# Opening of a fused attention and feed-forward kernel: the first two token tiles as one block, ten weight slices in plain float32 and six in two rounded parts

## The chip, the cores and the metric

The kernel runs on one core of one Trainium2 chip. The metric is the time of one execution on the device, in microseconds. The engines are named as in the profile: PE (TensorE, matmuls and transposes), PEld (its weight loads), DVE (VectorE), ACT (ScalarE), POOL (GpSimd), SP (the queue that issues nearly all transfers).

## The reference

For 8 batches and 8 heads with 512 local and 32 global tokens of width 64, global queries see all 544 keys; a local query sees the 32 global keys and the local keys at most 32 positions away. The result, with 8 x 64 = 512 columns and 8 x 544 = 4352 token rows, goes through a feed-forward layer of width 2048.

```python
s_g = scale * np.matmul(q_g, k_all.transpose(0, 1, 3, 2))
out_g = np.matmul(sm(s_g), v_all)
...
s_l = np.concatenate([s_lg, s_ll], axis=-1)          # s_ll masked to |i - j| <= 32
out_l = np.matmul(sm(s_l), np.concatenate([v_g, v_l], axis=2))
x = np.concatenate([out_g, out_l], axis=2).transpose(0, 2, 1, 3).reshape(B * S, H * D)
...
h = x @ w_in                                          # 512 -> 2048
out = (h * (1.0 / (1.0 + np.exp(-h)))) @ w_out        # 2048 -> 512
```

The weights come as 64-bit floats and are turned into 32-bit floats on the chip.

## The kernel before, in words

**Tiles and steps.** The 4352 rows are 34 token tiles of 128 rows (32 local ones, and two that collect the global rows of four batches each). A local tile takes two attention steps `k` (64 in all), each of four heads in two halves `i`. A step is scores (`sc`, L347), masked maximum (`mx`, L359), exponential (`ex`, L370), the reciprocal of the sum (`no`, L375 and L377), scaling of the probabilities (`sl`, L383 on DVE, L385 on ACT), transposes (`tu`, L419 plain, L421 of a rounded copy that a transfer makes, L391), copies out of them (`pt`, L433 on DVE, L435 on ACT), global probabilities put beside them (`pp`, POOL), values (`va`, L463), and the result copied to the layer's input tile (`xc`, L476; `xl` its rounding rest, L480). Global queries of a batch have their own chain: `gsc`, `gcp`, `gmx` (L262), `gex`, `gno` (L273), `gtu` (L291, L293), `pgt`, and for the first four steps `late` and `lc`.

**The layer.** Its 2048 inner columns are 16 slices `f`. The tiles form blocks (`SIZES`, 13 of them): 1, 1, 2 and then ten of 3. Blocks 0 and 1 run in plain float32: `one` (t, f) is four matmuls of 128 columns for one tile (L582), `th` the tanh (L586, ACT), `st` the rest of the activation (L592, DVE), `two` one matmul of 512 columns (L598). The trace shows each plain matmul as two instructions. From block 2 on, weights, inputs and inner values are split in a rounded upper and a lower part, and every product is the sum of three: upper by upper, and the two mixed ones. The first layer is twelve matmuls (L729) over all of a block's columns, the second three per tile (L751 to L753). Between them stand tanh (L735, ACT), L736 (DVE), the upper part (L738, ACT) and the lower part (L739, DVE). The second layer of a slice runs behind the first layer of the next one.

**Weights.** Each slice comes in two halves `w` (512 KB each, seven buffers), w_in's and then w_out's. A half is decoded by `js` (L186, DVE), `ja` (L182, ACT) and `jo` (L191, DVE), and split by `wh` (L209, ACT) and `wl` (L213, POOL).

**Order.** The opening's order over all engines is written out by hand in `START`, a list of words such as `sl3.1.0` (what, step, half, head pair). Each engine but PE is bound to the order in which it meets its words; PE's order is the program's. The words hold steps 0 to 8 of the attention, `w0` to `w31`, all of blocks 0 and 1 but the last `two` of both, the global chains of batch 0 and the scores and probabilities of batch 1, 24 matmuls that keep TensorE warm, and the splitting of slices 0 to 7. So it stands around the place of step 3:

```python
mx1.0 w5 ex0.1 mx1.1 w6 warm4 sc2 raw4 no0.0 raw5 ex1.0 no0.1 sl0.0.1 sl0.0.0 sl0.1.1 no1.0 sl0.1.0 warm5 tu0.0
...
sl2.0.0 no2.1 xc1 no3.0 warm2 tu2.0 sl2.1.1 sl2.1.0 one0.0 sl3.0.1 pt2.0 js2 sl3.0.0 js3 tu2.1 th0.0 pt2.1 tu3.0
ex3.1 st0.0 warm1 va2 js4 pt3.0 no3.1 ja2 js5 two0.0 sl3.1.1 xc2 jo2 sl3.1.0 ja3 js6 tu3.1 w9 one0.1 ja4 pt3.1
ja5 jo3 va3 th0.1 gcp0.0 jo4 w10 st0.1 xc3 one0.2 w11 jo5 ja6 gmx0.0 one1.0 w12 ja7 jo6 th0.2 two0.1 th1.0 ja8
```

After `START` the blocks from 2 on run slice by slice, and the remaining attention steps are put between their matmuls by due times: `at(k)` is the place of step `k` in the stream, `EARLY` how far ahead of it its predecessor's transposes stand (up to step 14), `ends` the places at which the blocks end, and `fill` moves on with every piece of the layer. `KF` (8) is the first step whose probabilities are rounded by a transfer before their transposes (`mv`, `st_move`, `g_move`). `AHEAD` (4) counts the first steps, which load queries and keys whole, with one transfer each (`st_load`); later ones use three.

Of the kernel before, what the change touches and what calls it, by code (L numbers as in the profile page):

```python
# [1 line left out]

# [45 lines left out]
raw0 raw1 v0 raw2 v1 w0 w1 raw3 v2 v3 warm6 sc0 g0.0.0 g0.0.1 w2 mx0.0 warm1 sc1 w3 g0.1.0 mx0.1 ex0.0 g0.1.1 w4  # L48
mx1.0 w5 ex0.1 mx1.1 w6 warm4 sc2 raw4 no0.0 raw5 ex1.0 no0.1 sl0.0.1 sl0.0.0 sl0.1.1 no1.0 sl0.1.0 warm5 tu0.0
js0 sl1.0.0 sl1.0.1 tu0.1 pt0.0 mx2.0 tu1.0 ex1.1 pt0.1 js1 warm1 va0 pt1.0 mx2.1 ja0 no1.1 sc3 ja1 sl1.1.1 jo0  # L50
xc0 sl1.1.0 jo1 w7 ex2.0 warm4 tu1.1 mx3.0 w8 gsc0.0 ex2.1 pt1.1 no2.0 va1 g1.0.0 ex3.0 mx3.1 g1.0.1 sl2.0.1
sl2.0.0 no2.1 xc1 no3.0 warm2 tu2.0 sl2.1.1 sl2.1.0 one0.0 sl3.0.1 pt2.0 js2 sl3.0.0 js3 tu2.1 th0.0 pt2.1 tu3.0
ex3.1 st0.0 warm1 va2 js4 pt3.0 no3.1 ja2 js5 two0.0 sl3.1.1 xc2 jo2 sl3.1.0 ja3 js6 tu3.1 w9 one0.1 ja4 pt3.1
ja5 jo3 va3 th0.1 gcp0.0 jo4 w10 st0.1 xc3 one0.2 w11 jo5 ja6 gmx0.0 one1.0 w12 ja7 jo6 th0.2 two0.1 th1.0 ja8
st0.2 w13 st1.0 gsc0.1 js7 gex0.0 js8 two1.0 jo7 gcp0.1 one1.1 gno0.0 w14 wh0.0 jo8 ja9 two0.2 wl0.0 w15 th1.1
gmx0.1 one1.2 wh0.1 st1.1 ja10 wl0.1 gtu0.0 js9 th1.2 js10 two1.1 gex0.1 st1.2 one0.3 jo9 pgt0.0 ja11 gno0.1
two1.2 w16 pp4.0 jo10 pp4.1 th0.3 ja12 late0 w17 one1.3 ja13 st0.3 v4 lc0 js11 wh1.0 gtu0.1 js12 th1.3 two0.3
jo11 wl1.0 ja14 pgt0.1 w18 one0.4 st1.3 jo12 ja15 pp5.0 late1 js13 th0.4 w19 two1.3 ja16 lc1 v5 st0.4 jo13 late2
wh1.1 two0.4 lc2 ja17 w20 wl1.1 js14 late3 js15 one1.4 jo14 wh2.0 lc3 w21 one0.5 jo15 th1.4 wl2.0 ja18 js16 sc4
w22 st1.4 th0.5 jo16 ja19 two1.4 raw6 st0.5 wh2.1 w23 mx4.0 two0.5 wl2.1 mx4.1 ex4.0 one1.5 js17 js18 ex4.1  # L60
one0.6 no4.0 jo17 sc5 th1.5 sl4.0.0 sl4.0.1 w24 st1.5 th0.6 tu4.0 raw7 no4.1 ja20 st0.6 two1.5 sl4.1.1 pt4.0
jo18 sl4.1.0 two0.6 js19 ja21 w25 mx5.0 tu4.1 ja22 one1.6 jo19 ex5.0 one0.7 pt4.1 w26 th1.6 mx5.1 ja23 va4 st1.6
th0.7 no5.0 ex5.1 st0.7 two1.6 pp5.1 v6 sl5.0.1 pp6.0 js20 xc4 two0.7 no5.1 sl5.0.0 xl4 sl5.1.0 one1.7 sl5.1.1
ja24 jo20 one0.8 ja25 js21 w27 th1.7 js22 tu5.0 ja26 st1.7 sc6 jo21 th0.8 pt5.0 two1.7 st0.8 w28 jo22 wh3.0 raw8
two0.8 js23 w29 wh3.1 wl3.0 mx6.0 one1.8 ja27 jo23 ex6.0 one0.9 wl3.1 mx6.1 w30 th1.8 tu5.1 js24 ja28 st1.8 sc7
pt5.1 th0.9 ex6.1 two1.8 st0.9 raw9 no6.0 jo24 wh4.0 two0.9 sl6.0.0 sl6.0.1 w31 wl4.0 one1.9 no6.1 ja29 js25
sl6.1.0 sl6.1.1 va5 jo25 th1.9 ja30 st1.9 one0.10 mx7.0 wh4.1 pp6.1 v7 mx7.1 xc5 pp7.0 two1.9 th0.10 wl4.1 xl5
ex7.0 one1.10 st0.10 js26 ex7.1 two0.10 no7.0 jo26 th1.10 one0.11 sl7.0.0 sl7.0.1 ja31 st1.10 tu6.0 no7.1 js27
th0.11 two1.10 pt6.0 sl7.1.1 st0.11 sl7.1.0 one1.11 jo27 wh5.0 js28 two0.11 th1.11 wl5.0 js29 wh5.1 st1.11 tu6.1
jo28 two1.11 pt6.1 wl5.1 one0.12 jo29 va6 js30 th0.12 wh6.0 js31 st0.12 one1.12 jo30 wh6.1 wl6.0 v8 xc6 jo31  # L70
two0.12 th1.12 xl6 pp7.1 tu7.0 st1.12 wl6.1 gsc1.0 pt7.0 two1.12 g1.1.0 gcp1.0 g1.1.1 tu7.1 gmx1.0 one0.13 wh7.0
pt7.1 one1.13 wh7.1 wl7.0 gex1.0 va7 th0.13 wl7.1 gno1.0 th1.13 gsc1.1 st0.13 xc7 xl7 two0.13 gcp1.1 st1.13
# [15 lines left out]
def attention_moe_kernel(ctx: ExitStack, tc: tile.TileContext, qk0_in, qk_in, v_in, gqk, wts, out):  # L88
# [122 lines left out]
    def w_rest(f, i):  # L211
        sl = slice(i * DM, (i + 1) * DM)
        nc.gpsimd.tensor_tensor(out=w_two[f][i], in0=w_32[f][:, sl], in1=w_hi[f][:, sl].bitcast(F32), op=ALU.subtract)  # L213
# [381 lines left out]
    def other(t, f):  # L595
        if f == 0:
            outs[t] = [ps_out.tile([P, DM], F32, tag=f"out{t}", name=f"out{t}")]
        nc.tensor.matmul(outs[t][0], g_slice(t, f), w_32[f][:, DM:], start=(f == 0), stop=(f == NF - 1))  # L598
# [121 lines left out]
    def first_layer(n, f):  # L720
        nt = SIZES[n] * P
        xh, xl = xblk[n]
        h = ps_h.tile([P, 512], F32, tag="h", name=f"h{n}_{f}")
        i = 0
        for c in range(NCC):
            wh = w_hi[f][:, c * P : (c + 1) * P]
            wl = w_lo[f][:, c * P : (c + 1) * P]
# [120 lines left out]
```

## Time and profile before

| | |
|---|---|
| median of three runs | 1013.99 us (1012.42 to 1014.07) |
| profiled execution | 1014.88 us |
| its span, first to last instruction | 1013.1 us |
| granted TensorE clock | 0.998 |
| first matmul of block 2 | 104.87 us after the span's start |
| PE, DVE, ACT, POOL busy | 1001.5, 492.4, 497.3, 85.6 us |

Times inside the profile are counted from the span's start. A TensorE instruction's duration holds its way through the array, which overlaps the next one's; the chain of work that ended last shows instead how far apart they stand. The bracket behind an instruction is idle time of its engine just before it, and what ended that.

### The profile page before, as it was taken

The page shows a single profiled execution, that of the slowest core. Times are in us where ns is not written, and L with a number is a line of the kernel's source. Part 1 is how long each engine was busy: PE and PEld are TensorE (multiplying, and loading weights), DVE is VectorE, ACT ScalarE, POOL GpSimd, SP SyncE. Part 2 cuts the span into 40 slices and gives each one's busy share as a digit, 9 for nine tenths or more (in the row PEclk, how much of TensorE's full clock was granted, in tenths as well). Part 3 has the DMA queues.
Part 4 walks back from the last instruction along what each step waited for, and adds up shares of the span by engine and source line. Part 5 has one row for each costly group of instructions (what it writes and reads, how often), then busy time and mean ns, then how long its engine had stood idle before and what let it go on. Part 6 is the DMA issues. An engine that isn't in the chain of part 4 may idle for free.

```text
span 1013.1 us, 17720 instructions
## 1 busy us (share of the span) xinstructions
PE 1001.5 (99%) x6280; PEld 860.8 (85%) x6280; DVE 492.4 (49%) x1634; ACT 497.3 (49%) x1332; POOL 85.6 (8%) x239
## 2 busy tenths in 40 slices
PE   8999999999999999999999999999999999999998
PEld 5776877888888888888888888888888888898997
DVE  6888455444544444453354444444444544433222
ACT  7776567444544554453354454445445543532322
POOL 1334054000000000000000000000000000000000
PEclk9999999999999999999999999999999999999999
DMA  9982434332423332332132333234224321300001
GB/s 338 348 283 81 156 105 154 127 104 92 132 84 117 103 110 86 112 114 68 46 126 89 116 95 110 93 114 135 71 81 146 102 82 58 106 32 1 32 1 32
DMA packets 85032, 110.97 MB, mean 110 GB/s; under 512 B 7760, under 2 KB 56144, under 8 KB 84944
## 3 DMA queue, kind: packets, MB, share of 16 engines
q1 hardware_dynamic: 84608, 109.38, 33.2%
q8 instruction: 50, 0.82, 0.3%
q10 hardware_dynamic: 336, 0.46, 0.1%
q14 instruction: 38, 0.31, 0.1%
HBM read 67.11 MB, written 8.91 MB: 75 GB/s over the span
## 4 chain that ended last, share of the span: by engine, by line
PE 90%; DMA 5%; DVE 2%; ACT 1%; POOL 0%; issue 0%; SPq 0%; POOLq 0%; ACTq 0%
PE h L729 34%; PE out L751 12%; PE out L752 11%; PE out L753 11%; PE o L463 7%; PE s L347 5%; PE t L421 3%; DMA raw_w<-in_wts_dram 3%; PE out L598 2%; PE h L582 2%; PE gs L251 1%; DMA rr<-probs 1%; DMA vraw<-in_v_dram 1%; PE gt L291 0%; DMA raw<-in_qk_dram 0%; POOL w_lo L213 0%
## 5 line engine op out<-in xcount | busy, mean ns | idle before, releaser
L729 PE MATMUL h<-xh,w_hi 128*128 128x384 f32 (+1 forms) x704 | 235.5, 335 | 0.0
L729 PE MATMUL h<-xh,w_lo 128*128 128x384 f32 (+1 forms) x704 | 233.9, 332 | 0.8 <-DMA w_lo<-w_lo 0.8
L729 PE MATMUL h<-xl,w_hi 128*128 128x384 f32 (+1 forms) x704 | 233.0, 331 | 0.0
L735 ACT ACTIVATE t<-h 128x384 f32<-128x384 f32 (+1 forms) x176 | 84.5, 480 | 272.8 <-PE h L729 272.2
L751 PE MATMUL out<-w_hi,gh 128*128 128x512 f32 x509 | 204.1, 401 | 0.0
L752 PE MATMUL out<-w_lo,gh 128*128 128x512 f32 x509 | 200.9, 395 | 0.0
L753 PE MATMUL out<-w_hi,gl 128*128 128x512 f32 x509 | 200.8, 394 | 0.0
L736 DVE SCALAR_TENSOR_TENSOR t<-t,h 128x384 f32<-128x384 f32 (+1 forms) x176 | 95.0, 540 | 211.6 <-ACT t L735 211.4
L739 DVE TENSOR_TENSOR gl<-t,gh 128x384 fp32r<-128x384 f32 (+1 forms) x176 | 98.1, 557 | 127.8 <-PE out L753 118.4
L729 PEld LDWEIGHTS h<-xh,w_hi 128*128 128x128 f32 x704 | 132.4, 188 | 11.1 <-issue 4.3
L729 PEld LDWEIGHTS h<-xl,w_hi 128*128 128x128 f32 x704 | 132.4, 188 | 6.9 <-issue 0.2
L370 ACT ACTIVATE probs<-probs,st 128x224 f32<-128x224 f32 x236 | 111.4, 473 | 49.4 <-DVE st L359 49.3
L729 PEld LDWEIGHTS h<-xh,w_lo 128*128 128x128 f32 x704 | 132.2, 188 | 1.0 <-DMA w_lo<-w_lo 1.0
L738 ACT CAST gh<-t 128x384 fp32r<-128x384 f32 (+1 forms) x176 | 88.4, 502 | 76.2 <-DVE t L736 75.1
L751 PEld LDWEIGHTS out<-w_hi,gh 128*128 128x128 f32 x509 | 95.6, 188 | 27.7 <-issue 13.3
L753 PEld LDWEIGHTS out<-w_hi,gl 128*128 128x128 f32 x509 | 95.5, 188 | 21.0 <-DVE gl L739 0.2
L752 PEld LDWEIGHTS out<-w_lo,gh 128*128 128x128 f32 x509 | 95.6, 188 | 14.2
L447 POOL COPY pt<-pgt 128x64 f32<-128x64 f32 x120 | 28.7, 247 | 743.3 <-PE o L463 432.4
L359 DVE CUSTOM_DVE_ANT_0 probs<-s,mask 128x224 f32<-128x224 f32 x236 | 78.3, 387 | 7.4 <-PE s L347 7.3
L463 PE MATMUL o<-pt,vraw 128*64 128x160 f32 (+1 forms) x1024 | 79.2, 297 | 0.1
L433 DVE COPY pt<-t 128x512 f32<-128x512 f32 x64 | 44.2, 691 | 64.5 <-PE t L421 62.0
L463 PEld LDWEIGHTS o<-pt,vraw 128*64 128x64 f32 x1024 | 62.9, 138 | 6.9 <-issue 2.0
(95 smaller groups left out, 971.4 us busy)
## 6 DMA issues: line engine op xcount, KB each, us to landing
rr<-probs SPq DMA_DIRECT2D x112, 256.0 KB, 2.4
vraw<-in_v_dram SPq DMA_DIRECT2D x64, 256.0 KB, 2.7
raw_w<-in_wts_dram SPq DMA_DIRECT2D x32, 512.0 KB, 6.7
raw<-in_qk_dram SPq DMA_DIRECT2D x59, 224.0 KB, 2.9
graw<-in_gqk_dram SPq DMA_DIRECT2D x32, 304.0 KB, 3.2
out_dram<-o SPq DMA_DIRECT2D x30, 256.0 KB, 2.1
raw<-in_qk_dram SPq DMA_DIRECT2D x118, 64.0 KB, 2.3
pgr<-pg SPq DMA_DIRECT2D x14, 272.0 KB, 2.6
```

Of the source, the lines that this page charges most:

```text
L347: nc.tensor.matmul(s[u][:, i * W : (i + 1) * W], raw[rows, q : q + P], raw[rows, key : key + W], start=True, stop=True)
L359: nc.vector.tensor_tensor_reduce(out=p[:, u, :W], in0=s[u][:, i * W : (i + 1) * W], in1=mask_of[c], scale=-SCALE, scalar=3.0e38, op0=ALU.a ...
L370: nc.scalar.activation(p[:, u, :W], p[:, u, :W], AF.Exp, bias=st[:, m : m + 1], scale=-1.0, accum_out=st[:, 4 + m : 5 + m])
L463: nc.tensor.matmul(o[D * u : D * (u + 1), i * wide : i * wide + m], vraw[:, i, a, u, :], pts[i][:, u, a, :m], start=(a == 0), stop=(a == 1))
L729: nc.tensor.matmul(h[:, :nt], wt, x[:, c, :nt], start=(i == 0), stop=(i == 3 * NCC - 1))
L735: nc.scalar.activation(t[:, :nt], h[:, :nt], AF.Tanh, scale=0.5)
L736: nc.vector.scalar_tensor_tensor(out=t[:, :nt], in0=t[:, :nt], scalar=1.0, in1=h[:, :nt], op0=ALU.add, op1=ALU.mult)
L738: nc.scalar.copy(out=gh[:, :nt], in_=t[:, :nt])
L739: nc.vector.tensor_tensor(out=gl[:, :nt], in0=t[:, :nt], in1=gh[:, :nt].bitcast(F32), op=ALU.subtract)
L751: nc.tensor.matmul(o, gh[:, sl], wh, start=(f == 0), stop=False)
L752: nc.tensor.matmul(o, gh[:, sl], wl, start=False, stop=False)
L753: nc.tensor.matmul(o, gl[:, sl], wh, start=False, stop=(f == NF - 1))
```

## The change

Blocks 0 and 1 become one block 0 of two tiles, and the block numbers after it fall by one. Its slices run in the order 6 to 15, then 0 to 5. Slices 6 to 15 stay in plain float32, tile by tile, with `one`, `th`, `st` and `two`. For slices 0 to 5 the input of both tiles is split (`fh`, ACT; `fl`, DVE), and the slice runs as it does in later blocks: `onr` (twelve matmuls of 256 columns), `thr`, `str`, `ghr`, `glr`, `twr` (three matmuls per tile), and adds to the same sums. The halves of the weights are loaded in the same order, `w12` to `w31` and then `w0` to `w11`. Scaling, the copies behind the transposes and the weights' lower parts name their engine in the word (A: ACT, V: DVE, P: POOL): scalings on DVE go from 18 to 14, those on ACT from 18 to 22; five of sixteen `wl` go from POOL to DVE. `nb` does the reciprocals of both halves of a step at once (steps 0, 4, 5, 6, 7). Steps 4 and 5 load whole. Step 8 and the global rows of batch 1 are transposed without the transfer that rounds them. `EARLY` falls, but for the transposes of step 8 the place moves to 0.4 ahead.

```diff
-SIZES = (1, 1, 2) + (3,) * 10
-PLAIN = 2
-AHEAD = 2 * PLAIN
+SIZES = (2, 2) + (3,) * 10
+AHEAD = 4
+WHOLE = 6
+
+PARTS = 6
...
 START = """
...
+raw0 raw1 v0 raw2 v1 w12 w13 v2 raw3 v3 warm6 sc0 g0.0.0 g0.0.1 w14 mx0.0 warm1 sc1 w15 g0.1.0 mx0.1 ex0.0
+g0.1.1 w16 mx1.0 w17 ex0.1 mx1.1 w18 warm4 sc2 raw4 raw5 ex1.0 nb0 mx2.0 slA0.0.0 slV0.0.1 slA0.1.0 no1.0 warm6
+tu0.0 slA0.1.1 js12 slA1.0.0 slV1.0.1 warm1 tu0.1 js13 ptA0.0 mx2.1 tu1.0 ex1.1 ptV0.1 ja12 ptV1.0 warm3 va0
+ja13 no1.1 jo12 slA1.1.0 sc3 xc0 slV1.1.1 w19 ex2.0 jo13 tu1.1 gsc0.0 mx3.0 w20 ex2.1 ptV1.1 g1.0.0 ex3.0 no2.0
+g1.0.1 warm2 va1 no2.1 slV2.0.1 slA2.0.0 slV2.1.1 slA2.1.0 no3.0 tu2.0 mx3.1 xc1 tu2.1 slA3.0.0 ptV2.0 one0.6
+ex3.1 ptV2.1 ja14 slV3.0.1 warm1 va2 no3.1 th0.6 js14 ja15 st0.6 tu3.0 slV3.1.1 slA3.1.0 jo14 two0.6 xc2 ptA3.0
+js15 w21 tu3.1 js16 ja16 one0.7 jo15 ptA3.1 jo16 w22 th0.7 va3 ja17 st0.7 w23 js17 gcp0.0 js18 two0.7 jo17 xc3
...
+ptV4.1 ex5.1 one0.14 jo1 va4 ja5 js2 w8 nb5 wh0.1 jo2 one1.14 th0.14 pp5.1 v6 xc4 slV5.0.1 pp6.0 w9 slA5.0.0
+st0.14 sc6 wlP0.1 xl4 th1.14 slA5.1.0 two0.14 st1.14 raw8 ja6 mx6.0 two1.14 wh1.0 slV5.1.1 js3 ja7 one0.15 js4
+ex6.0 jo3 one1.15 jo4 w10 th0.15 wh1.1 tu5.0 wlP1.0 st0.15 w11 mx6.1 th1.15 two0.15 ptA5.0 st1.15 ex6.1 onr0 js5
+js6 ja8 jo5 two1.15 ja9 jo6 thr0 tu5.1 js7 ja10 onr1 nb6 wlP1.1 str0 ptA5.1 ghr0 va5 jo7 slA6.0.0 wh2.0 glr0 sc7
+slV6.1.1 slA6.0.1 pp6.1 v7 js8 xc5 js9 pp7.0 twr0 wh2.1 raw9 xl5 wlP2.0 thr1 mx7.0 slA6.1.0 tu6.0 ja11 str1
+mx7.1 onr2 wlP2.1 ghr1 ptA6.0 ex7.0 glr1 tu6.1 jo8 sc8 wh3.0 jo9 thr2 twr1 wh3.1 wlV3.0 ptA6.1 str2 wlP3.1 onr3
+ex7.1 ghr2 js10 va6 wh4.0 glr2 nb7 thr3 wlP4.0 twr2 wh4.1 mx8.0 v8 xc6 str3 slA7.0.0 pp7.1 slV7.0.1 onr4 ghr3
+xl6 wlP4.1 slA7.1.0 mx8.1 slA7.1.1 tu7.0 ex8.0 glr3 gsc1.0 jo10 ptA7.0 no8.0 twr3 wh5.0 g1.1.0 js11 g1.1.1
+slV8.0.1 thr4 wlV5.0 ex8.1 tu7.1 str4 onr5 slA8.0.0 ptV7.1 ghr4 no8.1 gcp1.0 jo11 va7 slA8.1.0 glr4 slV8.1.1
+wh5.1 twr4 gmx1.0 xc7 wlP5.1 thr5 xl7 gex1.0 gsc1.1 str5 ghr5 gno1.0 wh6.0 glr5 gcp1.1 wlP6.0 wh6.1 gmx1.1
+wlV6.1 gex1.1 wh7.0 gno1.1 wh7.1 wlV7.0 wlV7.1
 """
...
-APART, EARLY = 6, 0.27
+APART, EARLY = 6, 0.1
...
-    def w_rest(f, i):
+    def w_rest(f, i, engine=nc.gpsimd):
...
-            if b:
+            if b > 1:
                 nc.tensor.transpose(o.bitcast(F32R), state["pgr", b, hh][:, sl], ident)
...
-        if k < AHEAD:
+        if k < WHOLE:
...
-            if k < KF:
+            if k <= KF:
                 nc.tensor.transpose(t[:, sl], p[:, sl], ident.bitcast(F32))
...
     def other(t, f):
-        if f == 0:
-            outs[t] = [ps_out.tile([P, DM], F32, tag=f"out{t}", name=f"out{t}")]
-        nc.tensor.matmul(outs[t][0], g_slice(t, f), w_32[f][:, DM:], start=(f == 0), stop=(f == NF - 1))
-        if f == NF - 1:
-            put_out(t)
+        if f == PARTS:
+            outs.setdefault(0, []).append(ps_out.tile([P, DM], F32, tag=f"out{t}", name=f"out0_{t}"))
+        nc.tensor.matmul(outs[0][t], g_slice(t, f), w_32[f][:, DM:], start=(f == PARTS), stop=False)
+
+    def first_upper(i):
+        if i == 0:
+            low = [two.tile([P, 2, 2 * P], F32R, tag="o", name=f"xl_first{j}") for j in range(2)]
+            xblk[0] = two.tile([P, NPR, 3 * P], F32R, tag="xh", name="xh_first"), low
+        nc.scalar.copy(out=xblk[0][0][:, 2 * i : 2 * i + 2, : 2 * P], in_=first[:, 2 * i : 2 * i + 2, : 2 * P])
+
+    def first_lower(i):
+        xh, low = xblk[0]
+        cs = slice(2 * i, 2 * i + 2)
+        nc.vector.tensor_tensor(out=low[i], in0=first[:, cs, : 2 * P], in1=xh[:, cs, : 2 * P].bitcast(F32),
+                                op=ALU.subtract)
...
+    def layer_products(n, f):
+        nt, (xh, xl) = SIZES[n] * P, xblk[n]
+        i = 0
+        for c in range(NCC):
+            wh = w_hi[f][:, c * P : (c + 1) * P]
+            wl = w_lo[f][:, c * P : (c + 1) * P]
+            low = xl[:, c, :nt] if n else xl[c // 2][:, c % 2]
+            for wt, x in ((wh, xh[:, c, :nt]), (wh, low), (wl, xh[:, c, :nt])):
+                nc.tensor.matmul(hs[n, f][:, :nt], wt, x, start=(i == 0), stop=(i == 3 * NCC - 1))
+                i += 1
...
+    def products(n, f, i):
+
+        gh, gl = gs[n, f]
+        sl, o = slice(i * P, (i + 1) * P), outs[n][i]
+        wh, wl = w_hi[f][:, DM:], w_lo[f][:, DM:]
+        nc.tensor.matmul(o, gh[:, sl], wh, start=(n > 0 and f == 0), stop=False)
+        nc.tensor.matmul(o, gh[:, sl], wl, start=False, stop=False)
+        nc.tensor.matmul(o, gl[:, sl], wh, start=False, stop=(f == (NF if n else PARTS) - 1))
+
+    def both(f):
+        for i in range(2):
+            products(0, f, i)
...
-            put(at(k) - EARLY, turns, k - 1)
+            put(at(k) - (EARLY if k > KF + 1 else 0.4), turns, k - 1)
...
-                put(at(k) + g["move"], g_move, b, hh)
                 put(at(k) + g["turn"], g_turns, b, hh)
                 if b > 1:
+                    put(at(k) + g["move"], g_move, b, hh)
...
-    pend = None
-    for n in range(PLAIN, len(SIZES)):
+    pend = 0, PARTS - 1
+    for n in range(1, len(SIZES)):
```

The functions `g_tanh`, `g_silu`, `g_upper` and `g_lower` (`thr`, `str`, `ghr`, `glr`) hold the four instructions of L735 to L739, unchanged but for the block's number. The last second-layer products of block 0 (slice 5) run behind the first `layer_products` of block 1.

More of the change, by code (lines that the diff above doesn't have):

```diff
@@ L47 @@
 START = """
[L48 to L72, printed above, removed]
@@ L528, in attention_moe_kernel @@
     first = two.tile([P, NPR, 3 * P], F32, tag="xl", name="x_first")
-    xblk = dict.fromkeys(range(PLAIN), (first, None))
+    xblk = {0: (first, None)}
     def xtiles(n):
@@ L612, in attention_moe_kernel @@
     does = dict(raw=st_load, v=st_vload, w=w_load, g=g_load, warm=warm, ja=w_upper, js=w_shift, jo=w_join,
-                sc=st_scores, mx=st_max, ex=st_exp, no=st_norm, sl=st_scale, tu=st_turn, pt=st_turned, pp=st_with,
+                sc=st_scores, mx=st_max, ex=st_exp, no=st_norm, nb=st_norm, sl=st_scale, tu=st_turn, pt=st_turned, pp=st_with,
                 va=st_values, xc=st_x, xl=lambda k: st_x(k, True), late=g_late, lc=g_late_add, gsc=g_scores, gcp=g_copy,
                 gmx=g_max, gex=g_exp, gno=g_norm, gtu=g_turn, pgt=g_turned, one=one, th=tanh,
-                st=silu, two=other, wh=w_cast, wl=w_rest, mv=st_move)
+                st=silu, two=other, fh=first_upper, fl=first_lower, onr=rows_of, thr=partial(g_tanh, 0),
+                str=partial(g_silu, 0), ghr=partial(g_upper, 0), glr=partial(g_lower, 0), twr=both, wh=w_cast, wl=w_rest)
+    for name in ("sl", "pt", "wl"):
+        for letter, engine in dict(A=nc.scalar, V=nc.vector, P=nc.gpsimd).items():
+            does[name + letter] = partial(does[name], engine=engine)
     traced, behind = nc.cur_bb.bb.instructions, {}
@@ L720, in first_layer @@
     def first_layer(n, f):
[L721 to L727, printed above, removed]
-            for wt, x in ((wh, xh), (wh, xl), (wl, xh)):
-                nc.tensor.matmul(h[:, :nt], wt, x[:, c, :nt], start=(i == 0), stop=(i == 3 * NCC - 1))
-                i += 1
-        t = two.tile([P, 3 * P], F32, tag="t", bufs=1, name=f"t{n}_{f}")
@@ new lines, in first_layer, with second_layer @@
+        layer_products(n, f)
+        for part in (g_tanh, g_silu, g_upper, g_lower):
+            part(n, f)
+    def second_layer(n, f):
+        if n and f == 0:
+            outs[n] = [ps_out.tile([P, DM], F32, tag=f"out{i}", name=f"out{n}_{i}") for i in range(SIZES[n])]
+        if (n, f) == (len(SIZES) - 1, NF - 1):
+            gh, gl = gs[n, f]
+            wh, wl = w_hi[f][:, DM:], w_lo[f][:, DM:]
+            for i, (g, w) in zip((0, 0, 1, 1, 2, 0, 2, 1, 2), ((gh, wh), (gh, wl)) * 2 + ((gh, wh), (gl, wh), (gh, wl)) + ((gl, wh),) * 2):
+                nc.tensor.matmul(outs[n][i], g[:, i * P : (i + 1) * P], w, start=False, stop=g is gl)
+        else:
+            for i in range(SIZES[n]):
+                products(n, f, i)
+                fill(1)
+        if f == (NF if n else PARTS) - 1:
@@ L771, in attention_moe_kernel @@
             fill(SIZES[n])
-            if pend is not None:
-                second_layer(*pend)
-            else:
-                for t in range(PLAIN):
-                    other(t, NF - 1)
-            pend = (n, f, *g)
+            second_layer(*pend)
+            pend = n, f
     second_layer(*pend)
```

98 lines of the change are left out of this document (54 added, 44 removed).

## The prediction

> **What bounds the kernel now.** I read the page first, then the table of stretches, then the groups by shape, the chain of waits between 25 and 121 us, and last the order of time of single engines where TensorE stood.
>
> ```profile
> span 1013.1 us, 17720 instructions
> PE 1001.5 (99%) x6280; PEld 860.8 (85%) x6280; DVE 492.4 (49%) x1634; ACT 497.3 (49%) x1332; POOL 85.6 (8%) x239
> ```
> ```profile
> 23.00:26.00 3.00, 1.42 (x8) 0.95 (x9) 1.61 (x5) 2.18 (x4) 0.00 (x0) 1.00 1.12 274
> 26.00:29.00 3.00, 3.00 (x24) 2.44 (x23) 3.00 (x7) 1.17 (x5) 0.00 (x0) 0.56 0.96 279
> ...
> 30.00:105.00 75.00, 74.01 (x501) 52.37 (x500) 60.98 (x186) 52.97 (x145) 27.79 (x32) 1.00 0.70 236
> ```
>
> The columns of a stretch are its length, then busy time of PE, PEld, DVE, ACT and POOL, the granted clock, the DMA share and GB/s. The page says that TensorE works for 99% of the span. Its matmuls overlap, so I trust the spacing in the chain more than the busy share. From 30 to 105 us (the rest of the opening, up to the first matmul of block 2 at 105 us) TensorE is busy 74.01 of 75 us at the full clock, and DVE 60.98 of 75. So the opening is bound by TensorE, with DVE at 81%, and every TensorE microsecond taken out counts as long as DVE keeps up. The exception lies before: 1.42 us busy of 3 from 23 us on, and then a clock of 0.56.
>
> **The change, part by part.** *Six slices in parts.* Now each of the 16 slices costs, for each of two tiles, one `one` (four matmuls, eight instructions) and one `two` (two instructions). After it, slices 6 to 15 stay so, and slices 0 to 5 become twelve matmuls of 256 columns and six of 512, which is what a slice of the present block 2 runs.
>
> ```profile
> 91.58 1.79 PE h L582 x16
> ...
> 95.52 1.91 PE out L598 x4
> ...
> 108.94 1.43 PE h L729 x12
> ...
> 111.76 0.24 PE out L752
> 112.00 0.23 PE out L753
> 112.23 0.24 PE out L751
> ```
> ```profile
> 34.16 0.89 PE h L582 x8
> 35.05 0.86 PE out L598 x2
> ...
> 80.16 0.44 PE t L419 x4
> ...
> 106.51 0.64 PE t L421 x8
> ```
>
> A plain slice for both tiles is 1.79 + 1.91 = 3.70 us where both tiles run together, and 2 x (0.89 + 0.86) = 3.50 where they alternate. In parts it is 1.43 + 6 x 0.235 = 2.84. The difference is 0.66 to 0.86 us; times six that is 4.0 to 5.2, and I take the middle, **-4.6 us**. The order keeps both patterns, so neither end is favoured. Nothing else hides this, since it is work taken off the bounding engine. The attention steps, the 24 warming matmuls and blocks 1 to 11 (2 and then 3 tiles, as blocks 2 to 12 now) keep their matmuls. Step 8 and the global rows of batch 1 now go through plain transposes (L419) instead of those of rounded copies (L421), and lose their DMAs on SP (`mv8.0`, `mv8.1`, two `g_move`). These are 8 + 10 transposes at 0.44 / 4 = 0.11 us instead of 0.64 / 8 = 0.08: **+0.5 us**; the four transfers were not waited for there, so their going is worth nothing.
>
> *The opening's order.* The hole at 23 us comes from the order.
>
> ```profile
> 20.81 1.09 PE L463 MATMUL o<-pt,vraw 128*64 128x128 f32 x16
> 21.84 1.13 PE L598 MATMUL out<-w,g_first 128*128 128x512 f32 x2
> 23.80 0.44 PE L419 MATMUL t<-ident,probs 128*128 128x128 f32 x2 [0.84 <-ACT probs L385]
> 24.86 0.44 PE L419 MATMUL t<-ident,probs 128*128 128x128 f32 x2 [0.61 <-DVE probs L383]
> 25.46 1.26 PE L582 MATMUL h<-x_first,w 128*128 128x128 f32 x8 [0.16 <-DVE w L191]
> 26.65 1.97 PE L463 MATMUL o<-pt,vraw 128*64 128x128 f32 x16
> ```
> ```profile
> 22.47 0.43 DVE L186 TENSOR_SCALAR raw_w<-raw_w 128x512 uint32<-128x512 uint32 x1 [1.52 <-DMA raw_w<-in_wts_dram]
> ...
> 23.01 0.17 DVE L377 RECIPROCAL st<-st 128x2 f32<-128x2 f32 x1
> 24.13 0.43 DVE L186 TENSOR_SCALAR raw_w<-raw_w 128x512 uint32<-128x512 uint32 x1 [0.95 <-DMA raw_w<-in_wts_dram]
> 24.47 0.33 DVE L383 TENSOR_SCALAR probs<-probs,st 128x224 f32<-128x224 f32 x1
> ```
>
> On DVE the shifts `js4` and `js5` wait 1.52 and 0.95 us for weights, and `no3.1` and `sl3.1.1`, which stand behind them, need no weight at all. TensorE waits for these to turn step 3. From 22.7 us (21.84 plus two times 0.43) to 25.46 it does 0.88 us of transposes: a hole of 1.9 us. The half clock then makes the values of step 3 last 1.97 instead of 1.09 us and the next `one`s 0.2 and some 0.7 longer: 1.8 us. Together 3.7 us could come back. In the new order `no3.1` stands ahead of `js14`, and `slV3.1.1` ahead of `jo14`, `js15` and `js16`, so step 3 is turned without waiting for the fifth weight half. What is late next: `ptA3.1` stands behind `ja16` on ACT, and that half lands at about 22.4 us (the 1.52 us wait ends there); `va3` then starts near 24 us, where 26.65 stands now. On SP, `raw4` and `raw5` go as one transfer each that waits for the scores of steps 0 and 1 alone, which sends the next weights off sooner but puts more bytes ahead of them. I take 2.2 of the 3.7 us: **-2.2 us**, ends 0 and -3.7, nearer the gain because the wait that made the hole is taken out of the way and a shorter one takes its place.
>
> The Trainium skill (TensorE: Matmul & The Clock Gate, "What's actually happening") says that the clock halves after about 3.4 us of idling and comes back after as long under load. The trace disagrees in the first half, since 1.9 us of waiting within 2.8 us sufficed; by the page alone the clock term would be a sure gain of 1.8 us, and by the row a hole of 1 us may still cost it.
>
> *What DVE, ACT and POOL get.*
>
> ```profile
> L739 DVE TENSOR_TENSOR gl<-t,gh 128x256 fp32r<-128x256 f32 x16 | 8.8, 548 | 5.4 <-ACT gh L738 2.7 <-PE out L753 1.9 <-ACT w_hi L209 0.8
> ...
> L736 DVE SCALAR_TENSOR_TENSOR t<-t,h 128x256 f32<-128x256 f32 x16 | 6.7, 418 | 12.0 <-ACT t L735 11.8
> ...
> L738 ACT CAST gh<-t 128x256 fp32r<-128x256 f32 x16 | 6.5, 404 | 3.6 <-DVE t L736 2.6 <-PE out L598 0.7
> ...
> L735 ACT ACTIVATE t<-h 128x256 f32<-128x256 f32 x16 | 6.0, 377 | 7.8 <-PE h L729 7.7
> ...
> L515 DVE TENSOR_TENSOR xl<-acc,xh 128x512 fp32r<-128x512 f32 x2 | 1.4, 688 | 0.2 <-ACT xh L514 0.2
> ```
> ```profile
> L383 DVE TENSOR_SCALAR probs<-probs,st 128x224 f32<-128x224 f32 x118 | 39.2, 333 | 1.6
> ...
> L262 DVE TENSOR_REDUCE gst<-pg 128x1 f32<-128x544 f32 x16 | 11.3, 709 | 1.1 <-ACT pg L256 1.1
> ...
> L592 DVE SCALAR_TENSOR_TENSOR g_first<-t_first,h 128x128 f32<-128x128 f32 x32 | 9.0, 281 | 5.4 <-ACT t_first L586 5.4
> L273 DVE TENSOR_SCALAR pg<-pg,gst 128x544 f32<-128x544 f32 x16 | 8.8, 551 | 0.6
> ```
>
> DVE gains `fl` (2 x 0.688), `str` and `glr` (6 x (0.418 + 0.548)) and five `wlV` (3.44), and loses twelve `st` (3.37) and four scalings to ACT (1.33). Five merged normalisations (two small instructions each, 0.17 a row above) take off 1.7: net +4.2 us. Of ACT's gain the largest part is 6 x (0.377 + 0.404) = 4.7 us, against 52.97 busy of 75 now: it has room, and I cost it at nothing but the seam below. On POOL five of the sixteen `wl` go. TensorE's part of the opening shrinks to some 68 us of the 75, and DVE's grows to 60.98 + 4.2 = 65.2. But `str5`, `glr5`, `gmx1.1`, `gno1.0`, `gno1.1` and three `wlV` stand behind the last TensorE word of the opening and run beside block 1: 0.97 + 0.71 + 2 x 0.55 + 2.06 = 4.8 us. That leaves 60.4 of 68, or 89%. Cover this thin is not whole: I put **+1.2 us** of new TensorE waits on it, between 0 (the present 81% cost it only 1 us in 75) and 4.6 (all of the first term).
>
> ```profile
> 47.69 1.83 POOL L213 TENSOR_TENSOR w_lo<-w,w_hi 128x512 fp32r<-128x512 f32 x1 [1.25 <-DVE w L191]
> ...
> 48.31 1.50 DVE L186 TENSOR_SCALAR raw_w<-raw_w 128x512 uint32<-128x512 uint32 x1
> ```
>
> A shift that takes 0.43 us elsewhere took 1.50 beside this POOL subtraction, so a `wl` on POOL costs DVE up to 1.07 us, and one moved to DVE costs it 0.69. The Trainium skill (SBUF — State Buffer, "Who interferes with whom") has DVE and GpSimd lock a shared port for a whole instruction; the trace agrees. By that rule the five moved `wl` would be a gain for DVE of 5 x 0.38 = 1.9 us at best instead of a cost of 3.44.
>
> *The seam.* The last products of block 0 now wait for `glr5`, which stands behind `gno1.0`, and that behind `gex1.0`; `gsc1.1` and block 1's first twelve matmuls (1.43 us) are the cover. Behind it, block 1's sums wait for the output copies of block 0, on an ACT that still has `wh6` and `wh7` to do. I take **+0.6 us**, ends 0 and 2.
>
> *The turns of steps 9 to 13* move from 0.27 to 0.1 units of the stream's time ahead of their group, that of step 8 to 0.4.
>
> ```profile
> PE t L421 <- DMA rr<-probs: 0.8, 2, 0.7
> ```
>
> TensorE waits for these transfers only 0.8 us between 105 and 175 us: gain at most 0.8, loss as much if the turned copies come late for the values. I take 0.
>
> Sum: -4.6 + 0.5 - 2.2 + 1.2 + 0.6 = **-4.5 us**. The profiled execution took 1014.88 us, 1.8 more than its span, and lies 0.9 above the median of 1013.99. On the median this gives **1009.5 us**.
>
> **The rivals.** *All of it comes back* (0.20): the hole and its clock go whole, DVE keeps pace, transfers are no longer waited for: -4.6 + 0.5 - 3.7 - 0.8 = -8.6, so 1005.4. For it speaks that each wait in the hole is one of order; against it, that DVE has less slack than before.
>
> *DVE becomes the bound* (0.18): if DVE can't do better than the 81% that it reaches now, its 60.4 us need 60.4 / 0.81 = 74.6 us instead of 75. The gain is then 0.4 us after 30 us and up to 2.2 before, some 1.3 in the middle, and 1012.7 the time. Against it: now TensorE, not DVE, sets the pace, so 81% is no limit of DVE's.
>
> *The split chain stalls TensorE* (0.10, slower): each slice in parts needs tanh, silu, upper and lower part in a row (0.377 + 0.418 + 0.404 + 0.548 = 1.75 us), each behind other work on two queues in order. The cover is the next `onr` and one attention piece, 1.43 + 1.0. With three strange instructions of 0.6 us in the way the chain takes 3.5 us, 1.1 over, six times: 6.6, and with no gain in the hole the time is 1014 - 4.6 + 0.5 + 6.6 = 1016.5. It decides from 4.1 / 6 = 0.68 us a slice on.
>
> **How the numbers follow.** My forecast (0.52) covers 1007 to 1011.9. A run of this kernel can tell 0.2% (2 us) from no change. Faster by more: forecast, first rival and a third of the second, 0.78; within, 0.12, the rest of the second; slower, 0.10. The range of 1004.5 to 1013.0 leaves out the slow rival and the edge of the first.
>
> **What would show it.** The first `h` of 12 matmuls of block 1 (two tiles, 256 columns) starts near 98 us, where 105 stands now; six runs of 12 before it take 1.44 us each. Between 22 and 30 us the clock stays over 0.9 and `va3` comes before 25 us. DVE is busy about 90% from 30 us to the seam. Wrong it would be if waits of `out` for `gl` or `gh` in the slices in parts add up to over 3 us, if block 1 loses more than 2 us in its first slices, or if the clock falls again.

## The result, and the profile after

| | before | after |
|---|---|---|
| median of five runs each | 1014.01 us (1012.42 to 1014.10) | 1005.78 us (1005.61 to 1006.38) |
| profiled execution | 1014.88 us | 1005.61 us |
| its span | 1013.1 us | 1003.8 us |
| first matmul of the first block that runs in parts throughout | 104.87 us | 96.85 us |
| first matmul of the first block of three tiles | 176.70 us | 167.46 us |

The changed kernel takes 0.9917 of the time before (95% interval 0.9906 to 0.9929), 8.2 us less. The prediction was 1009.5 us, 4.5 less. Of its cases the one that came nearest was a rival, "all of it comes back", at 1005.4 us.

The head of the page of the changed kernel:

```profile
span 1003.8 us, 17665 instructions
PE 994.9 (99%) x6266; PEld 859.9 (86%) x6268; DVE 490.9 (49%) x1626; ACT 501.1 (50%) x1339; POOL 76.8 (8%) x234
```

TensorE has 6.6 us less busy work and is still 99% busy. The time by stages shows where the gain arose. These are rows of TensorE's order of time (start, duration, line, tiles) in the two profiled executions, first of before and then of after, at the first matmul of three tiles:

```profile
176.70 0.33 PE L729 MATMUL h<-xh,w_hi 128*128 128x384 f32 x1
```
```profile
167.46 0.33 PE L635 MATMUL h<-xh,w_hi 128*128 128x384 f32 x1
```

They lie 9.24 us apart, and the spans 9.3: nothing changes behind this point. The profiled execution before was 0.87 us above its median and the one after 0.17 below, which is the distance to the 8.2 us of the medians. Of the 9.24 us, 8.02 stand already at the first matmul of the next block (104.87 and 96.85 us), so 1.2 more come within that block. One pair of traces does not settle these 1.2 us: in a second profiled execution of the changed kernel (the control below) that block takes 72.53 us, where it takes 71.83 in before and 70.61 in after.

The stretches that the prediction read, now of after (length, busy PE, PEld, DVE, ACT, POOL, granted clock, DMA share, GB/s):

```profile
23.00:26.00 3.00, 3.00 (x31) 2.47 (x30) 2.42 (x7) 2.59 (x7) 0.00 (x0) 1.00 1.05 390
26.00:29.00 3.00, 3.00 (x24) 2.40 (x24) 1.77 (x4) 0.89 (x3) 0.00 (x0) 1.00 1.03 401
30.00:97.00 67.00, 66.68 (x466) 50.14 (x467) 56.22 (x173) 54.89 (x146) 18.25 (x27) 1.00 0.70 240
```

The hole is gone (3.00 busy where 1.42 stood), the clock stays at 1.00, and the DMA engines move 390 and 401 GB/s where 274 and 279 stood. From 30 us to the seam TensorE is busy for 66.68 of 67 us, with DVE at 56.22, or 84%.

TensorE's order of time in after, with the places that the prediction named (`va3`, the seam, and the only waits above 0.2 us between 20 and 110 us):

```profile
24.41 1.09 PE L469 MATMUL o<-pt,vraw 128*64 128x128 f32 x16
...
30.10 1.16 PE L589 MATMUL h<-x_first,w 128*128 128x128 f32 x8 [0.69 <-DVE g_first L599]
...
96.85 0.36 PE L635 MATMUL h<-xh,w_hi 128*128 128x256 f32 x1
...
100.51 1.37 PE L352 MATMUL s<-raw 64*128 64x224 f32 x8 [0.41 <-ACT pt L441]
```

`va3` starts at 24.41 us (26.65 before), the next block at 96.85 (predicted near 98), and the seam costs one wait of 0.41 us.

The chain of work that ended last, in after: a plain slice of both tiles, and slices in parts.

```profile
51.50 1.91 PE out L605 x4
53.41 1.78 PE h L589 x16
...
81.72 1.43 PE h L635 x12
...
88.93 0.43 PE out L665
89.35 0.23 PE out L666
89.59 0.23 PE out L667
```

These are the durations that the first term was made of: 1.78 + 1.91 against 1.43 + 6 x 0.235, with 0.2 more for the first product where an attention piece stands before it.

### The profile page after: what moved, and what is told of

Read it like the earlier page. It is cut to its first block, busy times and chain, and to the rows that moved or that the text cites. A ratio compares the mean times of both kernels' runs of the same rounds, so it can differ in the third digit from the quotient of the medians.

```text
span 1003.8 us, 17665 instructions
## 1 busy us (share of the span) xinstructions
PE 994.9 (99%) x6266; PEld 859.9 (86%) x6268; DVE 490.9 (49%) x1626; ACT 501.1 (50%) x1339; POOL 76.8 (8%) x234
## 4 chain that ended last, share of the span: by engine, by line
PE 96%; DMA 1%; ACT 1%; DVE 1%; issue 1%; POOL 0%; POOLq 0%; ACTq 0%; DVEq 0%
PE h L635 36%; PE out L665 13%; PE out L666 12%; PE out L667 12%; PE o L469 7%; PE s L352 6%; PE t L427 3%; PE out L605 2%; PE gs L256 2%; PE h L589 2%; PE t L425 1%; PE gt L296 0%; PE idle L681 0%; DMA rr<-probs 0%; DMA raw<-in_qk_dram 0%
## 5 line engine op out<-in xcount | busy, mean ns | idle before, releaser
L642 ACT ACTIVATE t<-h 128x384 f32<-128x384 f32 (+1 forms) x182 | 86.8, 477 | 272.9 <-PE h L635 271.0
L665 PE MATMUL out<-w_hi,gh 128*128 128x512 f32 x521 | 209.3, 402 | 0.0
L666 PE MATMUL out<-w_lo,gh 128*128 128x512 f32 x521 | 205.6, 395 | 0.0
L667 PE MATMUL out<-w_hi,gl 128*128 128x512 f32 x521 | 205.5, 394 | 0.0
L646 DVE SCALAR_TENSOR_TENSOR t<-t,h 128x384 f32<-128x384 f32 (+1 forms) x182 | 97.4, 535 | 209.9 <-ACT t L642 209.8
L652 ACT CAST gh<-t 128x384 fp32r<-128x384 f32 (+1 forms) x182 | 90.8, 499 | 76.4 <-DVE t L646 76.2
L665 PEld LDWEIGHTS out<-w_hi,gh 128*128 128x128 f32 x521 | 97.8, 188 | 29.7 <-issue 14.5
L667 PEld LDWEIGHTS out<-w_hi,gl 128*128 128x128 f32 x521 | 97.7, 188 | 21.9 <-DVE gl L658 0.5
L666 PEld LDWEIGHTS out<-w_lo,gh 128*128 128x128 f32 x521 | 97.9, 188 | 14.5
```

Source lines behind the costliest of these rows:

```text
L642: nc.scalar.activation(t[:, :nt], hs[n, f][:, :nt], AF.Tanh, scale=0.5)
L646: nc.vector.scalar_tensor_tensor(out=t[:, :nt], in0=t[:, :nt], scalar=1.0, in1=hs.pop((n, f))[:, :nt], op0=ALU.add, op1=ALU.mult)
L652: nc.scalar.copy(out=gs[n, f][0][:, :nt], in_=gs["t"][:, :nt])
L665: nc.tensor.matmul(o, gh[:, sl], wh, start=(n > 0 and f == 0), stop=False)
L666: nc.tensor.matmul(o, gh[:, sl], wl, start=False, stop=False)
L667: nc.tensor.matmul(o, gl[:, sl], wh, start=False, stop=(f == (NF if n else PARTS) - 1))
```

## The experiments

The kernel before read medians of 1015.7 to 1016.2 us on the chips of these runs, so each experiment is told as its ratio to the kernel before on its own chip, and 0.001 is 1 us. The changed kernel itself, run again as a control, read 0.9916 [0.9902, 0.9929]; differences to it or to the kernel before are differences of these ratios. The brackets hold 95% intervals.

### Is the hole a matter of the order? Before with the new order, and after with the old one

```diff
  before, in START (b_order):
-... warm1 va2 js4 pt3.0 no3.1 ja2 js5 two0.0 sl3.1.1 xc2 jo2 sl3.1.0 ja3 js6 tu3.1 w9 one0.1 ja4 pt3.1
-ja5 jo3 va3 ...
+... warm1 va2 pt3.0 no3.1 ja2 two0.0 sl3.1.1 xc2 jo2 sl3.1.0 ja3 tu3.1 w9 one0.1 ja4 pt3.1
+jo3 js4 js5 js6 ja5 va3 ...
  after, in START (a_hole):
-... va2 no3.1 th0.6 js14 ja15 ... xc2 ptA3.0 js15 w21 tu3.1 js16 ja16 ... w23 js17 gcp0.0 ...
+... va2 js14 js15 js16 js17 no3.1 th0.6 ja15 ... xc2 ptA3.0 w21 tu3.1 ja16 ... w23 gcp0.0 ...
```

> The kernel before, with the shifts js4, js5 and js6 moved behind the last scaling and the last copy of step 3. Order theory: the hole of 1.9 us before step 3's transposes and the half clock behind it (1.8 us) go, so 1010.5 (-3.5 us), with the clock over 0.9 from 26 to 29 us. Rival (only the matmuls in parts count; TensorE meets the next wait for weights at once and stands there as long): 1013 to 1014.

> The changed kernel with the hole's cause put back: js14 to js17 stand on DVE ahead of the reciprocals and the last scaling of step 3, so these wait for the fifth and sixth weight halves. Order theory: a hole of 1 to 2 us at 22 us and a clock under 0.7 behind it, +3.3 us, 1009.1. Rival (TensorE catches up later because DVE sets the pace): 1006.

`b_order` read 0.9998 [0.9989, 1.0006]: nothing. `a_hole` read 0.9936 [0.9924, 0.9949], 2.0 us above the control, where 3.3 were expected. TensorE's order of time in `b_order`, and its stretches:

```profile
24.41 1.09 PE L463 MATMUL o<-pt,vraw 128*64 128x128 f32 x16
...
27.64 3.10 PE L582 MATMUL h<-x_first,w 128*128 128x128 f32 x16 [2.14 <-DVE w L191]
```
```profile
25.00:30.00 5.00, 2.86 (x24) 2.62 (x21) 3.79 (x9) 2.33 (x7) 0.00 (x0) 0.84 0.85 241
```

The order did what the prediction said of it: `va3` runs at 24.41 us, to the hundredth where the changed kernel has it. But the hole only moved. The next `one` waits 2.14 us for a decoded weight, the half clock follows, and the DMA engines move only 241 GB/s at a share of 0.85. The `one` needs the fifth weight half, `w4`. Its joining, `jo4`, stands behind `js6` on DVE, and `js6` waits for `w6`:

```profile
26.55 0.43 DVE L186 TENSOR_SCALAR raw_w<-raw_w 128x512 uint32<-128x512 uint32 x1 [0.97 <-DMA raw_w<-in_wts_dram]
```

So `b_order` is not the order of the changed kernel in full: there `jo16` (the fifth half again) stands ahead of `js17` and `js18`. The kernel before with that place changed too was not run; the nearest is `a_pieces` in the next section. In `a_hole` the transfers run as fast as in after (400 and 390 GB/s), and a hole comes all the same: `no3.1` and `st0.6` stand behind four shifts, two of which wait 1.10 and 0.86 us for weights to land. By these two, freeing step 3 from the shifts is needed, but it is not enough while the next work still stands behind a weight that has not landed.

### Why did the weights land late? The size of the loads of steps 4 and 5

On SP, before issues the next two weight halves (`w7` and `w8`) from 24.19 us on, after (`w19` and `w20`) from 18.45. The queue's order of time, of before and then of after:

```profile
22.47 0.38 SPq L323 DMA_DIRECT2D raw<-in_qk_dram  x1
24.19 2.02 SPq L172 DMA_DIRECT2D raw_w<-in_wts_dram  x2
```
```profile
18.45 1.16 SPq L177 DMA_DIRECT2D raw_w<-in_wts_dram  x2
```

The listing of the program before shows why. It gives SP's transfers eight semaphores in turn, and each transfer waits for the one that had its semaphore eight places earlier (the number in front is the place in SP's queue):

```
18 L172 DMA raw_w_199<-in_wts_dram 128x1024 [waits DMAHW1_49]
19 L172 DMA raw_w_206<-in_wts_dram 128x1024 [waits DMAHW2_49]
20 L322 DMA raw_219<-in_qk_dram 64x2x128 [waits DMAHW3_49]
...
25 L323 DMA raw_225<-in_qk_dram 128x2x224 [waits DMAHW0_49]
26 L172 DMA raw_w_301<-in_wts_dram 128x1024 [waits DMAHW1_49,DVE_49]
```

Steps 4 and 5 load in three pieces each before (two of 64 KB, one of 224 KB), so six of the eight transfers in flight are small. In the changed kernel each is one transfer, of 480 KB. Two kernels change this alone:

```diff
  before with the new order (b_order_whole = b_order and):
+WHOLE = 6
...
-        if k < AHEAD:
+        if k < WHOLE:
-            if k < 2:
+            if k % 4 < 2:
  after (a_pieces):
-WHOLE = 6
+WHOLE = 4
```

> The kernel before, with the shifts moved behind step 3 (as in b_order) and the inputs of steps 4 and 5 loaded whole, one transfer each instead of three. Slots theory: SP sends a transfer only when the eighth before it has landed, so the six small pieces delayed the weights that the hole moved on to; with both edits hole and half clock go: -3.5 us against before, transfers at 390 to 400 GB/s and the clock over 0.9 from 25 to 30 us. Rival (as in b_order, the next wait takes its place whatever is loaded): 0 to -1 us.

> The changed kernel, with the inputs of steps 4 and 5 loaded in three transfers each again. Slots theory: weights from the eighth half on come 5 us later, TensorE waits for them at 26 to 30 us: +2 to +3.5 us against the changed kernel, with a drop of GB/s from 20 to 30 us. Rival (the order alone made the early gain): 0 to +0.5 us.

> The changed kernel as it is, beside the next three on one chip. All theories: 8 us (0.8%) under the kernel before, whatever chip it is.

`b_order_whole` read 0.9973 [0.9963, 0.9984], 2.8 us faster than before (1013.12 against 1015.90 us) where this order alone gave nothing. `a_pieces` read 0.9935 [0.992, 0.995], 1.9 us above the control; the two intervals overlap, but the traces agree (below). Stretches from 25 to 30 us, of before, `b_order_whole` and `a_pieces`:

```profile
25.00:30.00 5.00, 4.84 (x33) 4.05 (x33) 4.54 (x10) 2.63 (x7) 0.00 (x0) 0.66 0.97 277
```
```profile
25.00:30.00 5.00, 3.93 (x32) 2.72 (x30) 3.59 (x9) 2.23 (x7) 0.00 (x0) 1.00 1.05 403
```
```profile
25.00:30.00 5.00, 4.53 (x38) 3.10 (x34) 2.98 (x7) 2.65 (x7) 0.00 (x0) 1.00 0.99 291
```

With whole loads the rate is 403 instead of 277 GB/s (after has 401 from 26 to 29 us), with pieces in the changed kernel 291. The wait that stays in `b_order_whole` is 1.1 us, and the clock holds:

```profile
PE h L583 <- DVE w L192: 1.1, 1, 1.1
```

(The columns are what waits and for whom, us in total, times, longest.) Of the 3.7 us that the prediction put on hole and clock, 3.7 - 1.1 = 2.6 should come back by this, and 2.8 did.

So the size of these loads costs time in both kernels. The account by slots, though, is not shown, and three rows speak against it as the whole cause. First, `w6`, which the hole of `b_order` waits for, has place 19, ahead of all six pieces, and was issued at about 15 us in both kernels; no slot held it up. Second, `w7`, the first weight behind the pieces, is issued at 24.80 us in `b_order` and at 19.10 in `b_order_whole`, 5.7 us earlier, but its decoding, which starts as it lands, starts only 0.65 us earlier (`b_order`, then `b_order_whole`):

```profile
29.79 0.67 ACT L182 ACTIVATE w<-raw_w 128x512 f32<-128x512 f32 x1 [2.54 <-DMA raw_w<-in_wts_dram]
```
```profile
29.14 0.68 ACT L183 ACTIVATE w<-raw_w 128x512 f32<-128x512 f32 x1 [2.76 <-DMA raw_w<-in_wts_dram]
```

Third, from 23 to 26 us the DMA engines are as busy with pieces as without (shares of 1.12 and 1.05), but with packets of 0.8 KB instead of 2.0 in the mean (before, then after):

```profile
DMA packets 1026, 0.82 MB, mean 274 GB/s; under 512 B 94, under 2 KB 982, under 8 KB 1025
```
```profile
DMA packets 582, 1.17 MB, mean 390 GB/s; under 512 B 40, under 2 KB 525, under 8 KB 581
```

Whether the pieces delay the weights by the slots that they take or by their small packets beside them was not told apart.

Nor does a low rate alone make the hole. In `a_pieces`, at 275 and 296 GB/s, TensorE does not stand still from 23 to 29 us and keeps its clock:

```profile
23.00:26.00 3.00, 3.00 (x30) 2.45 (x29) 2.09 (x6) 2.58 (x8) 0.00 (x0) 1.00 1.15 275
26.00:29.00 3.00, 3.00 (x24) 2.38 (x24) 2.31 (x5) 0.92 (x3) 0.00 (x0) 1.00 0.95 296
```

So the order of the changed kernel removes hole and half clock even with pieces. They cost it later: a `two` that starts at 42.97 us in after and at 42.91 in the control starts at 44.88 in `a_pieces`.

### What is a slice in parts worth? Three of the six plain again

```diff
  after, in START (a_plain3), for f = 0, 1, 2:
-onr0 ... thr0 ... str0 ... ghr0 ... glr0 ... twr0
+one0.0 one1.0 ... th0.0 th1.0 ... st0.0 st1.0 ... two0.0 two1.0
  and wh1.0 to wh3.1, wlP1.0 to wlP2.1 moved behind the plain slice
```

> The changed kernel, with slices 0, 1 and 2 in plain float32 again (three slices in parts instead of six; the splitting of weights 1, 2 and 3 stands a little later for it). Sum of the prediction: 3 x 0.77 = +2.3 us against the changed kernel. Rival (DVE sets the pace of the opening, so TensorE's work is not what counts): 0, or below, as each plain slice spares DVE 0.4 us. Rival (the chain of a slice in parts stalls TensorE): below +1.

It read 0.9942 [0.9929, 0.9954], 2.6 us above the control. Its chain, and its waits:

```profile
63.73 1.91 PE out L605 x4
65.64 1.78 PE h L589 x16
...
94.36 1.43 PE h L635 x12
```
```profile
PE h L635 <- DVE w_lo L218: 0.6, 1, 0.6
...
PE gs L256 <- DVE st L364: 0.3, 1, 0.3
```

In the traces its opening is 3.4 us longer; 0.9 of it are the two waits above, which after does not have. The other 2.5 us are 0.84 a slice, and 1.78 + 1.91 - 2.84 = 0.85 is what the durations give. So six slices are worth about 5.0 us, if the three that were not taken back give as much as the three that were. The time alone (2.6 us, with intervals of 1.3 on each side) agrees but would not give the second figure.

### The turns' places

```diff
  before (b_turns; b_ow_turns = b_order_whole and this):
-APART, EARLY = 6, 0.27
+APART, EARLY = 6, 0.1
-            put(at(k) - EARLY, turns, k - 1)
+            put(at(k) - (EARLY if k > KF + 1 else 0.27), turns, k - 1)
  after (a_turns):                     after (a_late):
-APART, EARLY = 6, 0.1                -APART, EARLY = 6, 0.1
+APART, EARLY = 6, 0.27               +APART, EARLY = 6, 0.01
```

> The kernel before, with the transposes of steps 9 to 13 at 0.1 instead of 0.27 units ahead of their group, and nothing else. Turns theory: the waits for the transfers of probabilities at 126.5, 147.5 and 168.5 us (0.7 to 0.8 us each beyond the usual spacing) shrink: -1.3 us, 1012.7. Rival (what I predicted, no effect): 1014.0.

> The kernel before with the edits of b_order_whole (-2.8 us there) and the transposes of steps 9 to 13 at 0.1 units. If the later transposes are worth in themselves what a_turns lost (3 us): -5.5 to -6 us against before, and no slice of block 2 waits for rr. Rival (their place fits only the changed opening, as b_turns gained nothing): -2.8 us. What then remains to the changed kernel is the price of slices in parts: 2.5 or 5 us.

> The changed kernel with the old 0.27 units for the transposes of steps 9 to 13 (step 8 stays at 0.4). Turns theory: +1.3 us, 1007.1, with waits of transposes for rr back in the trace. Rival (no effect): 1005.8.

> The changed kernel with the transposes of steps 9 to 13 at 0.01 instead of 0.1 units ahead of their group. Turns theory (what counts is the slack between a step's scores and its transposes; 0.27 cost 3 us in a_turns): 0 to -0.5 us against the changed kernel. Rival (the copies of the transposes come late for the values that follow): +0.5 to +1 us.

`b_turns` read 0.9998 [0.9989, 1.0007] and `b_ow_turns` 0.9976 [0.9964, 0.9987], where `b_order_whole` had 0.9973: in the kernel before, the later place gives nothing, with or without the hole. `a_late` read 0.9916 [0.9901, 0.993], as the control. `a_turns` read 0.9946 [0.9933, 0.996], 3.0 us above it: in the changed kernel the old place would cost. The waits of TensorE in `b_turns` from 94 us on, then a row of the order of time in `a_turns`:

```profile
PE out L751 <- ACT gh L738: 1.7, 1, 1.7
PE t L421 <- DMA rr<-probs: 1.0, 2, 0.7
```
```profile
141.92 0.54 PE L427 MATMUL t<-ident,rr 128*128 128x128 f32 x4 [2.22 <-DMA rr<-probs]
```

In `b_turns` the waits for the turned copies stay (1.0 us, 0.8 in before), and a new one of 1.7 us for an upper part comes in. In `a_turns` the copy is late by 2.22 us, and the clock is halved from 142.8 to 146.2 us (stretches of 1 us from 142 us on show 0.88, 0.50, 0.50, 0.50, 0.91), which costs 1.7 us more. The control waits 0.97 us at the same place at the full clock, so that 1.25 + 1.7 = 2.95 us are lost here, which is what the time shows (3.0). The two traces differ elsewhere too: over the whole block behind the seam `a_turns` takes 2.2 us more than the control (74.71 and 72.53).

### DVE and the seam

```diff
  after (a_pool):
-wlV3.0 ... wlV5.0 ... wlV6.1 ... wlV7.0 wlV7.1
+wlP3.0 ... wlP5.0 ... wlP6.1 ... wlP7.0 wlP7.1
  after (a_first_seam):
-gmx0.0 w24 ja19 one1.6 jo18 th0.8 w25 st0.8 gsc0.1 ja20 js19 th1.6 js20
+gmx0.0 w24 one1.6 th0.8 w25 st0.8 jo18 ja19 gsc0.1 th1.6 ja20 js19 js20
-wlV6.1 gex1.1 wh7.0 gno1.1 wh7.1 wlV7.0 wlV7.1
+wlV6.1 gex1.1 gno1.1
  (slice 7 is then split behind the opening, as the later slices are)
```

> The changed kernel with all sixteen lower parts of the weights on POOL again (the five wlV become wlP). Cover theory of the prediction (DVE at 89% is what threatens the opening; a lower part costs DVE 0.69 us itself and up to 1.07 us when POOL runs it beside a shift): little difference for DVE, and POOL's 1.3 us instead of 0.69 for the parts of slices 3, 5, 6 and 7: 0 to +0.7 us against the changed kernel. Rival (moving them to DVE was a load on the bound): -1 to -2 us.

> The changed kernel with two places eased. First, on ACT th0.8 and th1.6 stand ahead of the decoding of a half that is still on its way (ja19, ja20), and st0.8 ahead of jo18 on DVE. Second, the splitting of slice 7 is taken out of the opening's end and done by block 1's loop. Order theory: the 0.7 us wait of one for g_first near 30 us goes, and 0.4 to 0.6 us at the seam: -1.1 to -1.3 us against the changed kernel, the first part seen before 35 us, the second in block 1's first slices. Rival (TensorE meets the weights' landing at once, as in b_order): 0.

`a_pool` read 0.9908 [0.9893, 0.9923] and `a_first_seam` 0.9906 [0.9889, 0.9922]; neither can be told from the control. The decoding's shifts on DVE between 30 and 97 us (count, busy us, mean ns, idle before), in after, in `a_pool` and in the control:

```profile
L191 DVE TENSOR_SCALAR raw_w<-raw_w 128x512 uint32<-128x512 uint32 x25 | 12.4, 525 | 0.0
```
```profile
L191 DVE TENSOR_SCALAR raw_w<-raw_w 128x512 uint32<-128x512 uint32 x25 | 14.7, 614 | 0.0
```
```profile
L191 DVE TENSOR_SCALAR raw_w<-raw_w 128x512 uint32<-128x512 uint32 x25 | 15.1, 631 | 0.0
```

Five subtractions (3.4 us) leave DVE in `a_pool`, two of them in this stretch. Its 25 shifts take 2.3 us longer than in after, but in the control, which is the changed kernel itself, they take 2.7 us longer too; so this is a difference between executions, not one that the move to POOL made. TensorE waits 0.2 us for `st` between 30.5 and 97 us in `a_pool`, and 0.3 for a lower part on POOL. So neither side shows in the time. In `a_first_seam` both named waits of TensorE (0.69 and 0.41 us) are gone; DVE then waits 0.51 and 0.84 us for weights that have not landed, in the same place:

```profile
29.53 0.43 DVE L191 TENSOR_SCALAR raw_w<-raw_w 128x512 uint32<-128x512 uint32 x1 [0.51 <-DMA raw_w<-in_wts_dram]
...
30.79 0.43 DVE L191 TENSOR_SCALAR raw_w<-raw_w 128x512 uint32<-128x512 uint32 x1 [0.84 <-DMA raw_w<-in_wts_dram]
```

TensorE then waits 0.38 us at 32.07 us. So near 30 us the landing comes next behind the order, which fits the rival. Neither kernel (medians of 1006.64 and 1006.32 us) can be said to beat the changed one.

## Why the prediction was right or wrong

The direction was right and the time lies inside the range, but the size fell short by 3.7 us; the rival "all of it comes back" describes better what happened. By its terms:

- **Six slices in parts: -4.6, measured about -5.0** (twice what three showed). The mechanism and the rows held; the three save 0.84 each, the upper part of the 0.66 to 0.86.
- **Hole and clock: -2.2, measured -2.8** in `b_order_whole`, where a wait of 1.1 us stays. The size was near, the reason incomplete. The prediction laid the hole on DVE's order. That holds as far as it goes: with the order of the changed kernel hole and half clock are gone even with pieces (`a_pieces`), but freeing step 3 alone only moves the hole (`b_order`). It named the single transfers of steps 4 and 5 only as a source of earlier weights with more bytes ahead; they are worth another 1.9 us. The row to ask about was the DMA rate, 274 and 279 GB/s beside shares of 1.12 and 0.96, in a stretch in which the work waits for weights. By which way the pieces cost this stays open.
- **DVE's thin cover: +1.2, measured -0.7 to +0.3.** This is the term that failed most.

```profile
PE out L605 <- DVE g_first L599: 0.2, 1, 0.2
```

  That is all that TensorE waits in after between 30.5 and 97 us. In the control it is 1.2 us (two waits, one of 1.0), so executions differ; the three such waits of before between 30.5 and 105 us are 0.9. New waits are then -0.7 in the one and +0.3 in the other. DVE is at 84% (86% in the control), not 89: the sum of 60.4 us was 4 us too high. Most of that is the decoding, which the sum left as it was. The joining of the weight halves on DVE, in before, then after:

```profile
L191 DVE SCALAR_TENSOR_TENSOR w<-w,raw_w 128x512 uint32<-128x512 uint32 x32 | 24.6, 775 | 0.0
```
```profile
L196 DVE SCALAR_TENSOR_TENSOR w<-w,raw_w 128x512 uint32<-128x512 uint32 x32 | 21.3, 683 | 0.1
```

  It takes 3.3 us less, and as little in `a_pool` (21.3), so the subtractions moved off POOL are not the reason; what is was not tested. That a DVE at 84% costs nothing new fits what the second rival was denied for: TensorE, not DVE, sets the pace. That rival and the slow one (stalls of the split chain, 6.6 us) fall by the waits: no product of a slice in parts waits 0.2 us or more for `gh` or `gl` before the seam, in after or in the control.
- **The seam: +0.6, seen 0.41** as a wait, in another place than was named: scores wait for a copy behind the transposes on ACT, not products for `glr5` or sums for the output copies. It goes when the splitting of slice 7 leaves the seam (`a_first_seam`), so the load on ACT was read rightly, and the nearness of the size is partly luck. Without it the time is the same within what can be told.
- **The turns: 0, and the plain transposes: +0.5** (not run alone). In the kernel before the turns are worth 0 (two kernels). In the changed one they are not free: at the old place they cost 3.0 us. So the value belongs to the pair of opening and place, and costing the two apart could not show it.

The measured terms, -5.0 and -2.8, leave -0.4 of the 8.2 us for transposes, seam and turns together, where the prediction had +2.3 with DVE's cover. By the stages of the profiled pair what is left would lie in the block behind the seam (1.2 us), but the control does not repeat that. Its parts were not told apart: each is below what a time of this kernel resolves.

On the clock, the row that the prediction went by held: waits far shorter than the half clock itself brought it. What the runs add stands in the last section.

## What to carry to other kernels

Where an engine waits for work that itself waits for a load, freeing that work moves the wait to the next such place (`b_order`), so follow the order on to where nothing ready stands behind a load. Look also at the rate of transfers in that stretch, and if it is below what the kernel reaches elsewhere, try the small transfers around the large ones as one. A cover at 84% of an engine's time is enough if no single chain is late, so cost it by the waits that the trace shows, not by the share. Profile the same kernel twice before you lay a difference of 1 or 2 us between two traces on an edit. A place that was tuned in one order (the turns) can be worth nothing in another, so try it with the order that it goes with.
